# Linear attention and MoE block: two loads of each attention period are issued from ACT's queue instead of SP's

## Chip, cores, metric

One NeuronCore of a Trainium2 chip runs the whole program; the other cores are idle. The metric is the device time of one execution in microseconds (us). Engines are named as in the profile: PE (matmul), PEld (its weight loads), DVE (vector), ACT (scalar), POOL (GpSimd), SP (sync, issues transfers). "SPq" and "ACTq" are the instruction queues of SP and ACT where they issue transfers or wait.

## The reference

Linear attention over 8 batches of 8 heads (sequence 576, head size 64, 128 features), then a two-matrix feed-forward block (512 to 2048 to 512) over the 4608 rows that result.

```python
def phi(x):
    proj = einsum('bhsd,df->bhsf', x, w_phi)
    proj = proj - max(abs(proj), axis=-1, keepdims=True)
    return concatenate([exp(proj), exp(-proj)], axis=-1)
q_p, k_p = phi(q), phi(k)
kv  = einsum('bhsf,bhsd->bhfd', k_p, v)
z   = sum(k_p, axis=2)
num = einsum('bhsf,bhfd->bhsd', q_p, kv)
den = einsum('bhsf,bhf->bhs', q_p, z)[..., None] + 1e-06
attn = num / den
...
h = x @ w_in
out = (h - tanh(h)) @ w_out
```

The feed-forward weights come as 64-bit floats and are taken apart bit by bit on the core ("decoded") into 32-bit ones.

## The kernel before

The attention works on 32 units of two heads. A short ramp starts the first three; then `period(i)` runs for i = 3 to 31 (L808) and works on five units at once: it projects unit i, finishes the feature maps of i-1, sums and contracts i-2, takes numerator and denominator of i-3, and divides and stores i-4 and i-5. The order of the program is written out by hand: every engine and every queue executes its own instructions in the order in which the period names them, and waits are put in only where data or a buffer is not ready. Beside the units each period decodes one of 31 tiles of raw weights and prepares split weights for the feed-forward stage ("aside" work: subtractions on POOL, copies on ACT, stores `wd<-wr`). After period 31 a drain empties the pipeline, and the feed-forward stage, bound by matmuls, fills the rest of the time.

What one period issues on SP's queue, in order: `raw<-in_moe_w` (`dec_load`, L260 to L272, 512 KB, one of two buffers), `xs<-d` (`x_store`, the quotient of unit i-5, 288 KB, after POOL's multiplication `d<-d,rb` at L510), `qk<-in_qkT` (`load`, L300 to L303, 576 KB, one of two buffers), `dn<-dd` (`den_recip_load`, L492, the denominators of unit i-3 turned from rows into a column layout, 4.5 KB), two `rb<-rr` (`den_spread`, L507, the reciprocals broadcast over partitions), `v<-in_v` (320 KB), the stores of split weights, and `rr<-rn` (`den_store`, L502), which follows the reciprocal of the denominators on DVE (L497).

On ACT the middle of a period reads: `ksum_copy` (L432, the feature sums `kst`), `denom_copy` (L487, the denominators `dd`), copies `kv` (L449) and `ks` (L441), the first step of the decoding (`dec_0`, L279), copies of the weight preparation, the exponentials of q and k, `kvt` (L415), `num_copy` (L483). On DVE a period has the two steps of the feature maps' maxima (L345, L346), three further steps of the decoding (L283 to L291) and then the reciprocal (L497). On PE: projection (L327: `pj`, `pa`, `pt`), feature sums (L428), denominators (L470: `pu`), transposes (L445, L437, L356, L367), key-value product (L409), numerators (L456: `po`). The transposes at L367 write the part of bank `pu` that `denom_copy` has read.

The raw tile loaded in period i is used from L279 of period i+1 on, and its buffer is free after L291 of the period that uses it. The q and k loaded in period i are projected in period i+2, and their buffer is free when the projection of unit i in period i has ended.

Of the kernel before, what the change touches and what calls it, by code (L numbers as in the profile page):

```python
# [33 lines left out]
def tile_linear_attention_moe(  # L34
# [10 lines left out]
    nc = tc.nc  # L45
# [181 lines left out]
    with ExitStack() as c1:  # L227
# [32 lines left out]
        def dec_load(n, queue=nc.sync):  # L260
            u = Dec()
            kind, u.f = tiles[n]
            u.nm = f"{kind}{u.f}"
            u.d = wi if kind == "i" else wo
            u.r = raw.tile([P, DM], U64, tag="raw", name=f"raw{u.nm}")
            if kind == "i":
                queue.dma_start(
                    u.r.rearrange("p (c f) -> p c f", f=P),
                    w_in[:, u.f * P : (u.f + 1) * P].rearrange("(c p) f -> p c f", p=P),
                )  # L270
            else:
                queue.dma_start(u.r, w_out[u.f * P : (u.f + 1) * P, :])  # L272
            return u
# [26 lines left out]
        def load(u, queue=nc.sync):  # L300
            u.qk = pq.tile([P, PC], F32, tag="qk", name=f"qk{u.i}")
            for o, w in ((0, PC),) if u.i else ((5 * P, PC), (0, 5 * P)):
                queue.dma_start(u.qk[:, o:w], qkT[u.i][:, o:w])  # L303

        def load_v(u):
            u.v = pq.tile([P, 5, 2, D], F32, tag="v", name=f"v{u.i}")
            nc.sync.dma_start(u.v.rearrange("p j e d -> p (j e d)"), v5[u.i])


        def project(u, parts):  # L310
            for part in parts:
                if u.t is None:
                    u.t = [pq.tile([P, 2, 5, F], F32, tag="t0", name=f"t{u.i}_0"), None]
                    u.m = [p2.tile([P, 2, 5], F32, tag="m0", name=f"m{u.i}_0"), p2.tile([P, 2, 4], F32, tag="m1", name=f"m{u.i}_1")]
                if part == "j":
                    u.pj = ps_pj.tile([P, 2, 512], F32, tag="pj", name=f"pj{u.i}")
                    bank, tiles = u.pj, range(4)
                elif part == "t":
                    u.pt = ps_t.tile([P, 2, 512], F32, tag="pt", name=f"pt{u.i}")
                    bank, tiles = u.pt, range(4, 5)  # L320
                else:
                    u.pa = ps_d.tile([P, 2, 512], F32, tag="po", name=f"pa{u.i}")
                    bank, tiles = u.pa, range(5, 9)
                for k, a in enumerate(tiles):
                    for e in range(2):
                        hs = slice(e * D, (e + 1) * D)
                        nc.tensor.matmul(  # L327
                            bank[:, e, k * F : (k + 1) * F], u.qk[hs, a * P : (a + 1) * P], wph[hs, :], start=True, stop=True
                        )
# [10 lines left out]
        def centre(u, parts, h=None):  # L340
            for part in parts:
                x, m, t = part_of(u, part)
                if h is not None:
                    x, m, t = x[:, :, h], m[:, :, h], t[:, :, h]
                nc.vector.tensor_reduce(m, x, AX.X, ALU.max, apply_absolute_value=True)  # L345
                nc.vector.tensor_tensor(t, x, m.unsqueeze(3).broadcast_to(list(t.shape)), ALU.subtract)  # L346
# [48 lines left out]
        def k_exp(u, r, signs=(0, 1)):  # L395
            h, x, j = ((slice(SR, P), 4, 0), (slice(0, P), slice(0, 4), slice(1, 5)))[r]
            for s in signs:
                nc.scalar.activation(u.kp[h, :, j, s, :], u.t[r][h, :, x, :], AF.Exp, scale=1.0 - 2.0 * s)  # L398
# [18 lines left out]
        def kadd(u):  # L417
            x = p2.tile([P, 2, 2, F], F32, tag="ss", name=f"ss{u.i}")
            nc.gpsimd.tensor_tensor(x, u.kp[:, :, 1], u.kp[:, :, 2], ALU.add)
            nc.gpsimd.tensor_tensor(x, x, u.kp[:, :, 3], ALU.add)  # L420
            nc.gpsimd.tensor_tensor(x, x, u.kp[:, :, 4], ALU.add)
            nc.gpsimd.tensor_tensor(x, x, u.kp[:, :, 0], ALU.add)
            u.ss = x

        def ksum(u, x):
            u.pu = x
            for n in range(4):
                nc.tensor.matmul(x[n * 32 : (n + 1) * 32], ones, u.ss[:, n // 2, n % 2, :], start=True, stop=True)  # L428

        def ksum_copy(u):  # L430
            u.kst = p1.tile([P, F], F32, tag="kst", name=f"kst{u.i}")
            nc.scalar.copy(u.kst, u.pu)  # L432
# [31 lines left out]
        def denom(u, pu):  # L464
            u.pd = pu[:, F : F + CH]
            for s in range(2):
                for e in range(2):
                    for c in range(2):
                        n, w = 2 * e + c, 2 * e + s
                        nc.tensor.matmul(  # L470
                            u.pd[n * 32 : (n + 1) * 32, :],
                            u.ks[:, w * 32 : (w + 1) * 32],
                            u.qe[:, e, s, c * CH : (c + 1) * CH],
                            start=(s == 0),
                            stop=(s == 1),
                        )

        def num_copy(u):
            if u.i % 4 or u.i >= NU - 3:
                u.d = tail.tile([P, S], F32, tag="d", name=f"d{u.i}", bufs=3)  # L480
            else:
                u.d = p1.tile([P, S], F32, tag="d0", name=f"d{u.i}")
            nc.scalar.copy(u.d.rearrange("p (c n) -> p c n", c=2), u.po[:, :, 0:CH])  # L483

        def denom_copy(u):
            u.dd = pd.tile([P, CH], F32, tag="dd", name=f"dd{u.i}")
            nc.scalar.activation(u.dd, u.pd, AF.Identity, bias=bias_t[:, 3:4])  # L487

        def den_recip_load(u):
            w = 2 * S // P  # L490
            u.dn = tail.tile([P, w], F32, tag="dn", name=f"dn{u.i}")
            nc.sync.dma_start(u.dn, u.dd.rearrange("(n r) c -> n r c", r=32)[:, 0, :])  # L492
# [11 lines left out]
        def den_spread(u):  # L504
            u.rb = tail.tile([P, S], F32, tag="rb", name=f"rb{u.i}", bufs=1)
            for e in range(2):
                nc.sync.dma_start(u.rb[e * D : (e + 1) * D, :], u.rr[e : e + 1, :].broadcast_to([D, S]))  # L507

        def den_mul(u, pin=lambda ins: ins):
            pin(nc.gpsimd.tensor_tensor(u.d, u.d, u.rb, ALU.mult))  # L510

        def x_store(u):
            nc.sync.dma_start(xs[u.b // 2][u.hp, :, (u.b % 2) * S : (u.b % 2 + 1) * S], u.d)

        units = []
# [5 lines left out]
        NU = len(units)  # L521
# [7 lines left out]
        dec = []  # L529

        def unit(i):
            return units[i] if 0 <= i < NU else None

        def bank():
            return ps_c.tile([P, 512], F32, tag="pu", name="pu")
# [67 lines left out]
        def aside_at(i, late):  # L603
            for f in aside[i][late]:
                f()
# [56 lines left out]
        def period(i):  # L662
            a, c, p, r, q, o = (unit(i - n) for n in range(6))
            w = dec[i - 3]
            dec.append(dec_load(i - 2))
            if i > 3:
                num_copy(r)
            k_exp(c, 1)
            if o:
                den_mul(o)  # L670
                x_store(o)
            if i + 2 < NU:
                load(units[i + 2])
            project(a, "jat")
            centre(a, "jt")
            kadd(c)
            ksum(p, p.pc[:, 0:F])
            ksum_copy(p)
            pu = bank()
            denom(r, pu)  # L680
            denom_copy(r)
            den_recip_load(r)
            if q:
                den_spread(q)
            if i > 3:
                load_v(a)
            aside_at(i, 2)
            aside_at(i, 3)
            kv_turn(p)
            ksum_turn(p, p.pc[:, F : 2 * F])  # L690
            kv_turn_copy(p, nc.scalar.copy)
            ksum_turn_copy(p)
            dec_0(w, a.pt)
            if i < NU - 1:
                aside_at(i, False)
            aside_at(i, True)
            q_turn(c)
            q_turn_rest(c, pu)
            q_exp(c)
            q_exp_rest(c)  # L700
            centre(a, "a")
            k_exp(a, 0)
            kv(c)
            kv_copy(c)
            dec_1(w)
            dec_2(w)
            dec_3(w)
            if r:
                den_recip(r)
                den_store(r)  # L710
            num(p)
# [96 lines left out]
        for i in range(3, NU):  # L808
            period(i)
# [541 lines left out]
```

## Time and profile before

| | us |
|---|---|
| median of 3 runs | 1057.58 |
| range of the runs | 1056.92 to 1059.92 |
| profiled execution, its own time | 1059.23 |
| span of its instructions | 1057.4 |

The profile comes from one execution. Busy times are shares of the span; times in rows count from the span's start. An engine's idle time is listed with what ended it, as inferred from semaphores. A transfer's row is its issue; the landing is seen in the chain of waits or in who waits for it.

### The profile page before, as it was taken

Reading aid. Unit: us, or ns where it says so; the run is one execution under the profiler, and the core shown is the slowest. Engines: PE = TensorE matmul, PEld = TensorE weight load, DVE = VectorE, ACT = ScalarE, POOL = GpSimd, SP = SyncE. Lnnn points to the kernel's source line nnn. Section 1 sums busy time; section 2 is a strip of 40 time slices with the busy share of each in tenths; the row PEclk is TensorE's granted clock in tenths of the full one; section 3 lists DMA queues with packets and bytes.
Section 4 is the critical chain, followed back from the end, with each engine's and each line's share of the span. In section 5 each row is a group of like instructions: output and inputs, shape, how many; then the busy total and the mean of one; then the engine's idle time right before and its main releaser. Section 6 shows DMA issues by size and latency. Waiting matters only on the chain.

```text
span 1057.4 us, 19349 instructions
## 1 busy us (share of the span) xinstructions
PE 1042.4 (99%) x7484; PEld 874.0 (83%) x7484; DVE 870.2 (82%) x1086; ACT 792.1 (75%) x1281; POOL 272.8 (26%) x233
## 2 busy tenths in 40 slices
PE   8999999999989999999999999999999999999998
PEld 6666666666668998999999999999999999999997
DVE  7899888889979899878887788867887778877776
ACT  5888888988878778766777666776677667776665
POOL 4799899989960000000000000000000000000000
PEclk9999999999999999999999999999999999999999
DMA  5789999999847653464335433345334543353311
GB/s 166 205 233 282 264 271 288 267 272 270 253 142 263 201 187 103 159 216 144 121 120 190 167 131 122 120 169 179 128 106 156 199 137 113 120 180 109 123 47 60
DMA packets 75738, 184.59 MB, mean 175 GB/s; under 512 B 15744, under 2 KB 30464, under 8 KB 75648
## 3 DMA queue, kind: packets, MB, share of 16 engines
q1 hardware_dynamic: 75360, 183.17, 53.9%
q8 instruction: 59, 0.97, 0.4%
q14 instruction: 31, 0.25, 0.1%
q10 hardware_dynamic: 288, 0.20, 0.1%
HBM read 149.49 MB, written 33.70 MB: 173 GB/s over the span
## 4 chain that ended last, share of the span: by engine, by line
PE 82%; DMA 7%; DVE 5%; ACT 2%; POOL 2%; issue 1%; SPq 1%; ACTq 0%; DVEq 0%; POOLq 0%
PE A L142 18%; PE B L142 14%; PE po L987 12%; PE po L988 12%; PE po L993 12%; DMA dn<-dd 4%; PE po L456 3%; PE pc L409 3%; DVE t L346 2%; PE pj L327 2%; PE pa L327 2%; PE pu L470 2%; DVE m L345 1%; DMA rb<-rr 1%; DMA rr<-rn 1%
## 5 line engine op out<-in xcount | busy, mean ns | idle before, releaser
L142 PE MATMUL A<-xo,wr 128*128 128x384 f32 x1152 | 231.5, 337 | 0.0
L142 PEld LDWEIGHTS A<-xo,wr 128*128 128x128 f32 x1152 | 204.9, 188 | 11.4 <-ACT d L483 0.5
L911 ACT COPY u<-A 128x384 f32<-128x384 f32 x143 | 68.5, 479 | 142.6 <-PE A L142 142.2
L142 PE MATMUL B<-xo,wr 128*128 128x384 f32 x864 | 173.7, 337 | 0.0
L142 PEld LDWEIGHTS B<-xo,wr 128*128 128x128 f32 x864 | 152.5, 188 | 4.2 <-DVE hx L918 0.4
L987 PE MATMUL po<-who,ghx 128*128 128x512 f32 x288 | 112.3, 390 | 0.7 <-ACT hy L925 0.7
L987 PE MATMUL po<-who,ghy 128*128 128x512 f32 x288 | 112.3, 390 | 0.3 <-ACT ghy L962 0.3
L988 PE MATMUL po<-wlo,ghx 128*128 128x512 f32 x288 | 112.0, 389 | 0.0
L988 PE MATMUL po<-wlo,ghy 128*128 128x512 f32 x288 | 112.0, 389 | 0.0
L510 POOL TENSOR_TENSOR d<-d,rb 128x576 f32<-128x576 f32 x32 | 46.3, 1448 | 165.4 <-DMA rb<-rr 160.8
L950 DVE SCALAR_TENSOR_TENSOR s2y<-s2y,thy 128x768 f32<-128x768 f32 x48 | 46.0, 959 | 51.5 <-ACT thy L941 51.5
L398 ACT ACTIVATE kp<-t 64x256 f32<-64x256 f32 (+1 forms) x126 | 85.1, 722 | 2.1 <-DVE t L346 1.0
L993 PE MATMUL po<-who,glx 128*128 128x512 f32 x288 | 80.9, 389 | 0.0
L935 ACT ACTIVATE yx<-hx 128x768 f32<-128x768 f32 (+1 forms) x49 | 41.0, 836 | 52.9 <-DVE hx L918 52.9
L993 PE MATMUL po<-who,gly 128*128 128x512 f32 x282 | 79.3, 389 | 0.3 <-DVE gly L965 0.3
L409 PE MATMUL pc<-kp,v 128*64 128x256 f32 x640 | 76.1, 384 | 0.5 <-DMA v<-in_v 0.4
L456 PE MATMUL po<-qe,kv 128*64 128x288 f32 x512 | 69.0, 412 | 0.4
L993 PEld LDWEIGHTS po<-who,glx 128*128 128x128 f32 x288 | 54.0, 188 | 11.2
L947 DVE SCALAR_TENSOR_TENSOR s2x<-s2x,yx 128x768 f32<-128x768 f32 (+1 forms) x49 | 46.1, 941 | 20.4 <-ACT s2x L936 19.1
L993 PEld LDWEIGHTS po<-who,gly 128*128 128x128 f32 x282 | 52.8, 188 | 11.7 <-DVE gly L965 0.8
L987 PEld LDWEIGHTS po<-who,ghx 128*128 128x128 f32 x288 | 54.1, 188 | 8.8 <-ACT hy L925 1.1
L987 PEld LDWEIGHTS po<-who,ghy 128*128 128x128 f32 x288 | 54.1, 188 | 8.5 <-ACT ghy L962 0.7
(186 smaller groups left out, 2228.8 us busy)
## 6 DMA issues: line engine op xcount, KB each, us to landing
wr<-wd SPq DMA_DIRECT2D x92, 512.0 KB
wr<-wd SPq DMA_DIRECT2D x46, 768.0 KB
qk<-in_qkT SPq DMA_DIRECT2D x31, 576.0 KB
v<-in_v SPq DMA_DIRECT2D x32, 320.0 KB
rb<-rr SPq DMA_DIRECT2D x64, 144.0 KB
xs<-d SPq DMA_DIRECT2D x32, 288.0 KB
out<-o SPq DMA_DIRECT2D x35, 256.0 KB
rawi<-in_moe_w_in SPq DMA_DIRECT2D x16, 512.0 KB
```

The costliest lines, as they stand in the source:

```text
L142: nc.tensor.matmul(bank[:, 0:HT], w[:, a, n, cs], x[:, b, c, :], start=start and i == 0, stop=i == 5, skip_group_check=not start,)
L327: nc.tensor.matmul(bank[:, e, k * F : (k + 1) * F], u.qk[hs, a * P : (a + 1) * P], wph[hs, :], start=True, stop=True)
L398: nc.scalar.activation(u.kp[h, :, j, s, :], u.t[r][h, :, x, :], AF.Exp, scale=1.0 - 2.0 * s)
L409: nc.tensor.matmul(u.pc[e * D : (e + 1) * D, 0 : 2 * F], u.v[:, j, e, :], u.kp[:, e, j, :, :], start=(j == first), stop=(j == last))
L456: nc.tensor.matmul(u.po[e * D : (e + 1) * D, c, 0:CH], u.kv[:, s, e * D : (e + 1) * D], u.qe[:, e, s, c * CH : (c + 1) * CH], start=(s == ...
L510: pin(nc.gpsimd.tensor_tensor(u.d, u.d, u.rb, ALU.mult))
L911: nc.scalar.copy(t, A[q][:, 0:HT])
L947: nc.vector.scalar_tensor_tensor(z.s[:, s], z.s[:, s], GC, z.y[:, s], ALU.add, ALU.mult)
L950: nc.vector.scalar_tensor_tensor(z.s[:, s], z.s[:, s], GK, z.th[:, s], ALU.mult, ALU.mult)
L987: nc.tensor.matmul(po, z.gh[:, ts], wh, start=first, stop=False)
L988: nc.tensor.matmul(po, z.gh[:, ts], wl, start=False, stop=False)
L993: nc.tensor.matmul(po, z.gl[:, ts], wh, start=False, stop=last)
```

## The change

The two loads of a period leave SP's queue and the period's beginning; they are issued by ACT, after the copy of the feature sums and before the copy of the denominators. The loads of the ramp, the one in the drain, and all other transfers stay on SP's queue.

```diff
         def period(i):
             a, c, p, r, q, o = (unit(i - n) for n in range(6))
             w = dec[i - 3]
-            dec.append(dec_load(i - 2))
             if i > 3:
                 num_copy(r)
             k_exp(c, 1)
             if o:
                 den_mul(o)
                 x_store(o)
-            if i + 2 < NU:
-                load(units[i + 2])
             project(a, "jat")
             centre(a, "jt")
             kadd(c)
             ksum(p, p.pc[:, 0:F])
             ksum_copy(p)
+            dec.append(dec_load(i - 2, nc.scalar))
+            if i + 2 < NU:
+                load(units[i + 2], nc.scalar)
             pu = bank()
             denom(r, pu)
             denom_copy(r)
             den_recip_load(r)
```

## Rows read from the trace of the kernel before

**Rows 1.** The page, busy time of each engine over the span.
```profile
PE 1042.4 (99%) x7484; PEld 874.0 (83%) x7484; DVE 870.2 (82%) x1086; ACT 792.1 (75%) x1281; POOL 272.8 (26%) x233
```

**Rows 2.** Busy time by stretch: projection 3 to projection 31; then clock, DMA share, GB/s.
```profile
23.41:284.19 260.78, 256.89 (x3280) 172.70 (x3277) 234.63 (x310) 228.25 (x450) 229.88 (x194) 1.00 0.89 260
```

**Rows 3.** Timeline, PE: projections that open three periods (start us, us, instruction).
```profile
200.33 1.16 PE L327 MATMUL pj<-wph,qk 64*128 64x128 f32 x16
...
209.42 1.16 PE L327 MATMUL pj<-wph,qk 64*128 64x128 f32 x16
...
219.39 1.16 PE L327 MATMUL pj<-wph,qk 64*128 64x128 f32 x16
```

**Rows 4.** Waits of DVE, 30 to 300 us: total us, times, longest us.
```profile
DVE rn L497 <- DMA dn<-dd: 9.1, 11, 1.3
...
DVE rn L497 <- DMA v<-in_v: 2.2, 2, 1.6
DVE rn L497 <- DMA rb<-rr: 1.1, 2, 0.6
```

**Rows 5.** Timeline, DVE: the reciprocal in two periods, idle time before it in brackets.
```profile
201.43 0.21 DVE L497 RECIPROCAL rn<-dn 128x9 f32<-128x9 f32 x1 [0.46 <-DMA dn<-dd]
...
211.44 0.22 DVE L497 RECIPROCAL rn<-dn 128x9 f32<-128x9 f32 x1 [1.34 <-DMA dn<-dd]
```

**Rows 6.** Chain that ended last: two transfers of 4.5 KB (start us, us, what).
```profile
107.95 2.83 DMA rr<-rn
...
204.86 6.49 DMA dn<-dd
```

**Rows 7.** Timeline, SP: what one period issues, down to the broadcasts.
```profile
202.09 0.38 SPq L272 DMA_DIRECT2D rawo<-in_moe_w_out  x1
203.97 0.32 SPq L513 DMA_DIRECT2D xs<-d  x1
204.38 0.38 SPq L303 DMA_DIRECT2D qk<-in_qkT  x1
204.86 0.59 SPq L492 DMA_DIRECT2D dn<-dd  x1
205.54 3.18 SPq L507 DMA_DIRECT2D rb<-rr  x2
```

**Rows 8.** The page, DMA queues (q1 is SP's, q10 ACT's): packets, MB, share.
```profile
q1 hardware_dynamic: 75360, 183.17, 53.9%
...
q10 hardware_dynamic: 288, 0.20, 0.1%
```

**Rows 9.** Timeline, all engines: around the place of the new issues, and the raw tile's use.
```profile
200.29 0.69 DVE L291 SCALAR_TENSOR_TENSOR wi<-rawi,pt 128x512 uint32<-128x512 uint32 x1
...
202.22 0.39 PE L327 MATMUL pt<-wph,qk 64*128 64x128 f32 x4
...
203.11 0.25 ACT L432 COPY kst<-pc 128x128 f32<-128x128 f32 x1
...
204.05 0.50 ACT L487 ACTIVATE dd<-pu,bias_t 128x288 f32<-128x288 f32 x1 [0.70 <-PE pu L470]
...
204.89 0.28 PE L367 MATMUL pu<-ident,t 64*128 64x64 f32 x2
...
214.81 0.66 ACT L279 ACTIVATE pt<-rawo 128x512 f32<-128x512 f32 x1 [0.68 <-DVE t L346]
```

**Rows 10.** Line 487: ACT's queue waiting for the denominators; ns min/median/max.
```profile
L487 ACTq EVENT_SEMAPHORE  x31: 616/895/2111, 35.8 to 308.5; - x31
```

**Rows 11.** Line 303: issue of a q, k load on SP; ns min/median/max.
```profile
L303 SPq DMA_DIRECT2D qk<-in_qkT x33: 328/383/929, 0.7 to 270.9; - x33
```

**Rows 12.** Waits of SP's queue, 30 to 300 us: total us, times, longest us.
```profile
SPq L272 <- DMA qk<-in_qkT: 2.5, 3, 1.1
```

**Rows 13.** Timeline, SP: a q, k load and the raw load eight issues after it.
```profile
243.86 0.38 SPq L303 DMA_DIRECT2D qk<-in_qkT  x1
...
250.12 0.33 SPq L272 DMA_DIRECT2D rawo<-in_moe_w_out  x1
```

## The prediction

> **What bounds the kernel now.** Three views, in this order. First the page's busy times: PE is busy for 99% of the span [rows 1], so time can only come from where PE stands. Then the stretch of the attention: the 28 periods from the projection of unit 3 to that of unit 31 take 260.78 us [rows 2], 9.31 us each. The timeline gives the length of single periods, from one projection to the next [rows 3]: 9.09 us from 200.33 to 209.42, 9.97 us from 209.42 to 219.39. A period issues the same matmuls each time, and 9.09 is the shortest that I find, often repeated; I take it as PE's floor. 28 x 9.09 = 254.5, so 260.78 - 254.5 = 6.3 us is all that better feeding can give here. Of the other resources DVE works 234.6 of those 260.8 us, POOL 229.9, ACT 228.3, and the DMA engines are 0.89 busy at 260 GB/s [rows 2]: all close behind PE.
>
> Third, what makes a period long. DVE stops at the reciprocal of the denominators, L497, until `dn` has landed: 9.1 + 2.2 + 1.1 = 12.4 us in 15 periods [rows 4] (the releaser named differs, the waiting line is one; I count all three as the same wait). Behind the reciprocal, in DVE's order, stand the maxima of the next projection, then the transposes on PE and the first decoding step on ACT. A wait of 0.46 us opened the period of 9.09, one of 1.34 us the period of 9.97 [rows 3, 5]. So some 0.48 us of such a wait is hidden and the rest lengthens the period (1.34 - 0.88 = 0.46 gives the same). 12.4 - 15 x 0.48 = 5.2 us of the 6.3 belong to late denominators, at least, since waits under 0.48 subtract too much.
>
> Why `dn` is late: it is 4.5 KB, and took 6.49 us in the chain, where `rr`, as small, took 2.83 [rows 6]. All but 0.2 MB of the program's 183 MB goes through one queue, SP's [rows 8], and on it `dn` stands behind the raw tile, `xs` and q, k [rows 7]: 512 + 288 + 576 = 1376 KB, 5.4 us at 260 GB/s.
>
> **The change, part by part.**
>
> *SP loses two issues.* The q, k issue holds SP from 204.38 to 204.76, and `dn` follows at 204.86 [rows 7]; two such places make 0.48 x 2 = 0.96 us of SP's time per period. `dn` can follow `xs` directly, 0.4 us earlier, if `dd` is there (it ended at 204.55 [rows 9]; so 0.3 here). The broadcasts, `v` and the stores move up with it. SP is not the bound, so by itself this gives only that.
>
> *The transfers on two queues.* On SP's queue `dn` has only `xs` of this period ahead: 288 KB are 1.1 us at the full 260 GB/s, 2.3 at half of it. No row shows two loaded queues side by side, so I bound it. Below: `dn` lands as soon as `rr` does plus that, 2.83 + 1.1 to 2.83 + 2.3, or 3.9 to 5.1 us, 1.4 to 2.6 us sooner than 6.49. Above: the 16 engines take the same bytes in the same order, and nothing is sooner. I take the upper half of the gain, since the two loads wait in a ring of their own. Then a gain of 1.4 covers nearly every wait (1.6 is the longest [rows 4]), and 5.2 us come back. Even a third of it, 0.5 us, would bring back more than half, because only what exceeds 0.48 counts.
>
> The Trainium skill (DMA: Bandwidth & Descriptors, Issuing engines are not separate DMA queues) speaks against this: transfers from different engines run on the same 16 DMA engines, and issuing from several saves only issue time. By it the sum would hold nothing but SP's issue time, a rival below. The same page (Queues, rings and completion order) says that each DMA engine goes round between the queues packet by packet, which would be the gain; no run here shows it yet.
>
> *The loads start later or earlier.* The raw tile goes from 202.09 to some 203.2, 1.1 us later, and its first user comes at 214.81 [rows 7, 9]: 11.6 us, where even the 6.49 us transfer would do. Cost nothing; if it took over 11.6 us, ACT would stop there. q and k go from 204.38 to some 203.7, for a projection two periods on. Cost nothing.
>
> *Waits taken to ACT.* Raw needs the buffer that DVE's L291 frees (200.98), q and k the one that PE's `pt` frees (202.61); both are over before `kst` starts at 203.11 [rows 9]. Behind the issues on ACT stand `dd`, then `kv`, `ks`, decoding and exponentials; PE's L367 overwrites what `dd` reads and ran 0.34 us after `dd` had ended [rows 9].
>
> *ACT's time.* ACT is busy 228.25 / 28 = 8.15 us of a period; two issues as on SP (0.48 each, of which 0.383 is the instruction [rows 11]) make 9.11, over the floor, if they exclude work. They need not: ACT's queue already begins to wait for the denominators as `kst` starts, for 895 ns in the median [rows 10], so it runs ahead of the copy. 0.96 us in a hole of 0.895 makes `dd` 0.07 us late, 28 x 0.07 = 1.9 us if every period passes it on, nothing if L367's slack takes it. I take 1.0. If ACT's queue does not run ahead past an issue, the hole is 0.70 us [rows 9], `dd` is 0.26 late, and 7.3 us is the upper end.
>
> **Sum.** 5.2 - 1.0 = 4.2 us. The profiled execution took 1059.23 us, its span 1057.4; so 1055.0 against its own time, and as it lies 1.65 above the median of 1057.58, 1053.4 us against the median. What lies behind the attention starts earlier and is not touched.
>
> **Rivals.**
>
> *All of it comes.* Every period falls to 9.09 and ACT passes nothing on: 6.3 us, 1051.3. For it: POOL and ACT also wait for what is late now. Against: DMA engines near their limit. Chance 0.10.
>
> *The order on the DMA engines stays.* Raw, `xs`, q and k still pass before `dn`, only from two rings; raw starts 1.1 us later, which takes back what SP's shorter queue gives. 1057.6, with 1 us on ACT at most 1058.6. For it: DMA engines 0.89 busy, so the bytes ahead decide. Against: `dn` waits for 1376 KB of which 1088 leave its queue. Chance 0.25.
>
> *Slower: an issue holds ACT until an old load has landed.* SP's raw issues waited three times for the landing of q, k, up to 1.1 us [rows 12]. In each the q, k load was the eighth transfer before: from 243.86 come `dn`, two `rb`, `v`, two `xo`, `rr`, and raw is the eighth at 250.12 [rows 13]. So an issue waits for the eighth before it, and this one landed after about 6.2 us. In the new order a period with one store has raw as eighth after the last q, k load: ACT would wait there, with `dd` and PE behind. It has some 8.6 us for it (9.09 - 0.48). It decides where q, k, sharing the engines, takes longer than that. Each 0.1 us per period costs 2.8 us; more than 0.26 us on average eats the 4.2 and another 3.2. With 0.3 us: 8.4 - 4.2 = 4.2 us slower, 1061.8. For it: the loads are the largest, with engines 0.89 busy. Against: 2.4 us to spare. Chance 0.20.
>
> **How the numbers follow.** A measurement of this kernel tells about 0.3% from no change, 3.2 us: faster is under 1054.4, slower over 1060.8. Forecast (0.45) and the first rival (0.10) are faster, but the forecast lies only 1.0 us inside, so I leave 0.03 of it to "same": faster 0.52, same 0.28, slower 0.20. The forecast's own range is 1051.3 to 1055.5. The range given goes from 1051.0 to 1060.5: it holds the first three cases, and leaves out most of the slow one.
>
> **What would show it.** Right: q10 carries some 30 MB; DVE's wait at L497 shrinks from 12.4 to under 3 us; periods of 9.09 to 9.2; `dn` lands in 4 to 5 us; `dd` starts within 0.1 us of `pu`'s end as now. Wrong: waits at L497 as before (second rival); ACT idle at L487 or its queue longer than 0.9 us, with PE waiting at L367 (third); a raw tile late at L279.

## The result, and the profile after

The changed kernel takes **1067.45 us** (median of 4 runs, 1066.42 to 1068.43); the kernel before, run beside it, 1058.21 (4 runs, 1056.92 to 1059.92). The ratio is 1.0086, with a 95% interval of 1.0067 to 1.0105: some 9 us slower. The forecast was 1053.4 with a range of 1051.0 to 1060.5; the sign is wrong, and the time lies outside the range.

The profiled execution took 1066.42 us, its span 1064.6, against 1057.4 before: 7.2 us more. The page of the changed kernel answers [rows 1, 8]: PE is as busy as it was, and some 31 MB have gone from q1, SP's queue, to q10, ACT's.

```profile
PE 1044.1 (98%) x7484; PEld 875.3 (82%) x7484; DVE 870.4 (82%) x1086; ACT 791.6 (74%) x1281; POOL 272.3 (26%) x233
...
q1 hardware_dynamic: 61536, 152.04, 43.4%
q10 hardware_dynamic: 14112, 31.33, 10.3%
```

The stretch of the 28 periods, from the projection of unit 3 to that of unit 31 (columns as in [rows 2]: length, busy time of PE, PEld, DVE, ACT, POOL, clock, DMA share, GB/s):

```profile
23.52:291.94 268.42, 258.53 (x3280) 173.86 (x3277) 234.61 (x310) 227.05 (x450) 230.02 (x195) 1.00 0.85 252
```

It grew from 260.78 to 268.42 us, by 7.64: the whole loss of the profiled execution lies here. The granted clock is at its full 2.4 GHz in both, and no engine works more than PE's 1.6 us longer than before. The DMA engines are less busy, 0.85 against 0.89: they have the same bytes and more time.

Waits of the changed kernel, 30 to 300 us (total us, times, longest us), answering [rows 4]:

```profile
POOL d L510 <- DMA rb<-rr: 20.5, 19, 3.5
DVE rn L497 <- DMA dn<-dd: 13.3, 13, 1.7
...
DVE rn L497 <- DMA v<-in_v: 5.4, 3, 2.3
...
DVE rn L497 <- DMA rb<-rr: 2.6, 2, 1.4
```

POOL's wait for the broadcasts was 11.7 us in 16 periods before. The wait that was to vanish has grown: 13.3 + 5.4 + 2.6 = 21.3 us in 18 periods, after 12.4 in 15. The prediction's rule, that 0.48 us of each is hidden and the rest lengthens the period, still counts right: 21.3 - 18 x 0.48 = 12.7, less the 5.2 of before is 7.5, against the 7.64 measured. So what has to be explained is why the denominators are later.

The chain of waits of the changed kernel (start us, us, what), for the transfers that answer to `dn` in [rows 6]:

```profile
202.50 6.14 DMA dn<-dd
...
212.56 5.72 DMA dn<-dd
```

They are about as slow as the 6.49 us of before, although raw, q and k have left their queue. Over the 28 periods, from issue to landing, the median of `dn` went from 5.08 to 5.83 us and that of `xs` from 3.52 to 6.27 (worked out from the updates of the transfers' semaphores in the two traces). One period shows how. SP's timeline (start us, us, instruction), then ACT's:

```profile
212.15 0.32 SPq L513 DMA_DIRECT2D xs<-d  x1
212.56 0.59 SPq L492 DMA_DIRECT2D dn<-dd  x1
213.88 1.11 SPq L507 DMA_DIRECT2D rb<-rr  x2
215.08 0.54 SPq L307 DMA_DIRECT2D v<-in_v  x1
```

```profile
210.39 0.27 ACT L432 COPY kst<-pc 128x128 f32<-128x128 f32 x1
210.49 0.33 ACTq L272 DMA_DIRECT2D rawo<-in_moe_w_out  x1
210.92 0.39 ACTq L303 DMA_DIRECT2D qk<-in_qkT  x1
211.36 0.50 ACT L487 ACTIVATE dd<-pu,bias_t 128x288 f32<-128x288 f32 x1 [0.70 <-DVE t L346]
```

And the DMA queues (packets, MB, share of the 16 engines) in three stretches of this period: 212.2 to 215.2, 215.2 to 216.7 and 216.7 to 217.7 us:

```profile
q10 hardware_dynamic: 174, 0.68, 78.9%
q1 hardware_dynamic: 10, 0.00, 0.2%
...
q10 hardware_dynamic: 99, 0.37, 60.7%
q1 hardware_dynamic: 108, 0.23, 38.7%
...
q1 hardware_dynamic: 272, 0.28, 104.9%
```

`xs` is on q1 from 212.15 on, `dn` from 212.56 on. For 3 us q1 moves nothing of them, while q10 moves raw and the first of q, k. For 1.5 us the two queues share. `dn`'s 36-byte packets come after 216.7, with the last of `xs`. So raw and q, k, issued first, are still ahead of `xs` and `dn`; a second queue is no way past them.

The other periods are alike. By the sizes of the packets in the two traces, `xs` has its first packet 0.92 us after its issue before (median) and 3.24 us after it now. Raw's first packet, on q10, came ahead of that of `xs`, on q1, in all 26 periods that store `xs`, and q, k's in 23 of 25.

On ACT's side, answering [rows 11, 10], the q, k issues and the queue's waits for the denominators:

```profile
L303 ACTq DMA_DIRECT2D qk<-in_qkT x27: 334/517/1447, 26.7 to 277.0; - x27
L487 ACTq EVENT_SEMAPHORE  x9: 17/17/2099, 37.2 to 315.8; - x9
```

A q, k issue takes 0.52 us here, up to 1.45, and the queue stops for the denominators 9 times, where it was 31 times before: the two issues fill the hole. Idle time before `dd`, summed over the 28 periods, grew from 18.8 to 24.0 us.

### The profile page after: what moved, and what is told of

Its sections match the earlier page's. It is cut to its first block, busy times and chain, and to the rows that moved or that the text cites. A ratio compares the mean times of both kernels' runs of the same rounds, so it can differ in the third digit from the quotient of the medians.

```text
span 1064.6 us, 19312 instructions
## 1 busy us (share of the span) xinstructions
PE 1044.1 (98%) x7484; PEld 875.3 (82%) x7484; DVE 870.4 (82%) x1086; ACT 791.6 (74%) x1281; POOL 272.3 (26%) x233
## 3 DMA queue, kind: packets, MB, share of 16 engines
q10 hardware_dynamic: 14112, 31.33, 10.3%
## 4 chain that ended last, share of the span: by engine, by line
PE 73%; DMA 12%; DVE 5%; ACT 4%; POOL 4%; issue 1%; SPq 1%; ACTq 1%; POOLq 0%; DVEq 0%
PE A L142 18%; PE B L142 14%; PE po L987 12%; PE po L988 12%; PE po L993 12%; DMA dn<-dd 4%; DMA rb<-rr 3%; DMA rr<-rn 2%; DVE t L346 2%; DMA xs<-d 2%; DVE m L345 2%; PE po L456 2%; ACT kp L398 1%; PE pc L409 1%; POOL d L510 1%
## 5 line engine op out<-in xcount | busy, mean ns | idle before, releaser
L409 PE MATMUL pc<-kp,v 128*64 128x256 f32 x640 | 76.1, 384 | 0.8 <-ACT ks L441 0.2
L993 PEld LDWEIGHTS po<-who,gly 128*128 128x128 f32 x282 | 52.9, 188 | 11.7 <-DVE gly L965 0.7
L409 PEld LDWEIGHTS pc<-kp,v 128*64 128x64 f32 x640 | 43.4, 136 | 22.0 <-ACT ks L441 1.8
```

The lines of the kernel that those rows point to most:

```text
L409: nc.tensor.matmul(u.pc[e * D : (e + 1) * D, 0 : 2 * F], u.v[:, j, e, :], u.kp[:, e, j, :, :], start=(j == first), stop=(j == last))
L993: nc.tensor.matmul(po, z.gl[:, ts], wh, start=False, stop=last)
```

## The experiments

**The theories**, by the letters of the expectations. P: what is issued first passes first, on either queue; at first q, k were taken for what delays `xs` and `dn`. T (from e5 on): it is raw, issued later, that pushes back everything issued after it. Q: a second queue costs something itself. A: the two issues hold ACT. L: an issue is held until an old load has landed (the slower rival, in whatever queue it turns up).

Medians are set against runs of the kernel before beside them (medians of 1060.05 to 1060.43 us). "28 periods" below is the stretch of [rows 2], from each trace's timeline, and "L497" the sum of DVE's waits there, 30 to 300 us. A trace is one execution: e6 and e17 are the same kernel, and their 28 periods took 258.46 and 256.04 us, so a difference of 2 us between two traces says little.

**e1_lanes.** In the waits of SP's queue the changed kernel has 28.5 + 15.3 us behind the landing of `xs`, which was not so before:

```profile
SPq L502 <- DMA xs<-d: 28.5, 11, 4.2
...
SPq L112 <- DMA xs<-d: 15.3, 6, 3.4
```

As in [rows 12, 13], the transfer waited for is the eighth before: the trace has the program's transfers on eight semaphores in turn, 62 issues each. Naming `xs` between the two loads moves it by one in that count and alters nothing else:

```diff
-                x_store(o)
...
             dec.append(dec_load(i - 2, nc.scalar))
+            if o:
+                x_store(o)
             if i + 2 < NU:
```

> The changed kernel with the store of xs named between the two loads. SP's and ACT's queues hold the same instructions in the same order; only the count of transfers, by which each issue waits for the eighth before it, is as in the kernel before (raw, xs, q k, dn). Theory L (the loss comes from SP's issue of rr and of weight stores waiting until xs, now the eighth before them, has landed: 28.5 + 15.3 us of such waits in the changed kernel): these waits fall under 10 us in total and the time returns to 1056 to 1060 us. Theory P (the loss comes from the order in which the DMA engines serve: q and k are now issued ahead of xs and dn and pass first, whatever queue they are on): xs still lands 6 us after its issue, DVE's wait at L497 stays near 20 us, time 1064 to 1068. Theory A (the two issues hold ACT): as the changed kernel, 1067.

Measured: 1070.61, ratio 1.0103 [1.0067, 1.0139]; 28 periods 273.93. The waits did not move (26.2 us in 9 and 16.0 in 6), so it could not test L, and the time did not come back.

**e2_raw and e3_qk** do one half of the change each: only raw, or only q, k, on ACT behind `ksum_copy`.

```diff
-            dec.append(dec_load(i - 2))
...
+            dec.append(dec_load(i - 2, nc.scalar))
```

> Only the raw load moves to ACT, at the new place; q and k stay on SP behind xs. Theory P: xs goes ahead of q and k again and lands in 3.5 to 4.5 us, dn stands behind the same transfers as before: 1056 to 1061 us. Theory L: xs is the eighth before rr in periods with one store here too, but counts only if xs lands late: between 1058 and 1064. Theory A: half of ACT's load of issues, some 1063.

> Only q and k move to ACT, at the new place; the raw load stays first on SP. The count of eight is as in the kernel before. Theory P: q and k are issued some 0.7 us ahead of xs and pass first, xs lands 2 to 3 us later than before, dn no sooner than before: 1060 to 1067. Theory L: no new wait for xs at rr, 1056 to 1060. Theory A: some 1063 from one issue on ACT per period.

Raw alone: 1068.73, ratio 1.0082 [1.0053, 1.0112]. q, k alone: 1059.77, 0.9996 [0.9972, 1.0019]. The whole loss is raw's. This is outside every range given for e2, and P had it the other way round, the loss with q, k. DVE's wait with raw alone, and SP's with q, k alone:

```profile
DVE rn L497 <- DMA dn<-dd: 20.0, 17, 2.2
```

```profile
SPq L502 <- DMA xs<-d: 16.8, 10, 2.5
```

With q, k on ACT `xs` lands late too (6.65 us), and SP waits for it eight transfers on; the time stays. With the waits for raw, SP is held before `rr` for 25.7 us in 18 periods in e3, without a loss, and for 27.7 us in 17 in e2, with all of it. So L falls as the cause. A falls with e2: the idle time before `dd` is 18.5 us there, no more than the 18.8 before.

**e4_dn_first** leaves raw in place and moves q, k on SP's queue behind `dn`. If `dn` alone were the matter, this should bring back the 5.2 us of the prediction.

```diff
-            if i + 2 < NU:
-                load(units[i + 2])
...
             den_recip_load(r)
+            if i + 2 < NU:
+                load(units[i + 2])
```

> The kernel before with q and k issued directly behind dn instead of ahead of it, all on SP. Theory P: dn and xs no longer stand behind 576 KB, dn lands about 2 us sooner (5.1 to 3 us in the median), DVE's wait at L497 goes from 12.4 to under 4 us, time 1052 to 1056. If the denominators are late for another reason than the bytes ahead of them (no theory that counts on order holds): 1057 to 1060. Theories L and A say nothing against 1058.

Measured: 1060.76, ratio 1.0012 [0.999, 1.0034]. DVE no longer waits at L497 at all, the 28 periods took 259.01 us in the profiled execution, 1.8 less than before, and yet the runs show no gain. `v` is late in its stead (PE waits 2.3 us for it, 0.4 before), and POOL's wait for the broadcasts stays (11.7 us in 16 before), with longer single waits (1.8 at most before):

```profile
POOL d L510 <- DMA rb<-rr: 11.0, 10, 3.7
PE pc L409 <- DMA v<-in_v: 2.3, 2, 1.5
```

Behind the periods this execution lost 1.6 us again: PE waited there 3.1 us at once for POOL's sums (L422; 1.5 and 1.1 us in two waits before), and from 296.7 us on it was granted 1.2 GHz for 3.4 us.

**e5_place_sp** issues both loads at the change's place, but on SP's queue (first diff, against the changed kernel); **e6_raw_early** goes the other way, raw on ACT earlier than before, between the two halves of the exponentials, with q, k on SP untouched (second diff, against the kernel before).

```diff
-            dec.append(dec_load(i - 2, nc.scalar))
+            dec.append(dec_load(i - 2))
             if i + 2 < NU:
-                load(units[i + 2], nc.scalar)
+                load(units[i + 2])
```

```diff
-            dec.append(dec_load(i - 2))
...
-            k_exp(c, 1)
+            k_exp(c, 1, (0,))
+            dec.append(dec_load(i - 2, nc.scalar))
+            k_exp(c, 1, (1,))
```

> The change's places in the program, but both loads on SP's queue: SP then issues rr, xs, raw, q k, dn, so raw starts some 2 us later than before and dn stands directly behind both. Theory T (what costs is that the raw load starts later, after the DMA engines have run dry, so that what dn stands behind passes later; the queue's name does not matter): as slow as the changed kernel or slower, 1066 to 1080. Theory Q (a second queue itself costs, the place does not): 1056 to 1061.

> The raw load on ACT, but issued between the two exponentials of k that open ACT's part of the period, about 0.9 us into it instead of 2.9 (1.9 in the kernel before); q and k stay on SP as before. Theory T: not slower than before, 1054 to 1061, DVE's wait at L497 at or under 12.4 us. Theory Q: raw on ACT's queue costs as with raw alone at the late place, 1065 to 1070.

e5: 1086.21, ratio 1.0251 [1.0216, 1.0286]; on SP the place puts raw behind SP's own waits, 5.4 us into the period. e6: 1057.83, 0.9973 [0.9949, 0.9998], faster than the kernel before. So Q falls: ACT's queue is not at fault, and at the same place in the program it is better than SP's. On ACT's queue raw's place alone makes the difference between 0.8% lost (e2) and 0.3% gained (e6).

**e8_qk_after_v and e10_raw_late_dn_free** were to show that raw's lateness costs through `dn` alone: q, k go behind `v`, out of everyone's way, first by itself and then with raw late as in e2.

```diff
-            if i + 2 < NU:
-                load(units[i + 2])
...
                 load_v(a)
+            if i + 2 < NU:
+                load(units[i + 2])
```

> The kernel before with q and k issued on SP behind dn, both rb and v. With q, k directly behind dn the wait at L497 went to nothing and v came late instead (PE's L409 waited). Theory of order (each transfer passes in the order of issue; q and k have two periods of slack, everything else has none): no wait at L497, none for v, 1051 to 1056. If something other than late transfers sets the 0.16 us over the floor: 1057 to 1061.

> Raw on ACT at the change's late place, as in the run that was 0.8% slower, but q and k behind v on SP, out of dn's way. If raw's lateness costs only through dn's landing, the loss goes: 1052 to 1060, no wait at L497 to speak of. If it costs in another way (raw itself late for the decoding, ACT held): 1065 or more.

Both missed. e8: 1064.92, ratio 1.0046 [1.0029, 1.0062]; e10: 1078.35, 1.0179 [1.0125, 1.0233]. In e8 `rr` now passes behind q, k, and SP stops for it with the broadcasts in hand:

```profile
SPq L507 <- DMA rr<-rn: 48.2, 22, 3.4
```

Against e8, raw's lateness costs 1.3% here too, though L497 has only 17.7 us; PE waits 8.8 us for `v`, and part of the loss is the clock (see below). None of the places tried for q, k was out of everybody's way.

**e11_both_raw_early** is the change with raw at e6's place; **e12_no_raw** is the change without the periods' raw loads (all tiles are decoded from the first raw tile, so it leaves out 512 KB a period).

```diff
             u.d = wi if kind == "i" else wo
+            if n:
+                u.r = dec[0].r
+                return u
```

> The changed kernel with the raw load moved up between the two exponentials of k that open ACT's part of the period (0.7 us into it instead of 2.9); q and k stay on ACT at the change's place. Theory T (the raw load's start is the whole loss): not slower than the kernel before, 1055 to 1061. If q and k on ACT, or two issues on ACT, cost something of their own, which raw's lateness hid: 1062 to 1068.

> The changed kernel without the raw loads of the periods: every weight tile is decoded from the first raw tile, so 512 KB a period are not loaded, while q and k stay on ACT at the change's place and all arithmetic is done. Theory T: with these bytes gone nothing is late, periods go to the floor of 9.09 us, wait at L497 under 4 us, 1050 to 1057. If ACT's issue of q and k or the new order among the others (xs behind q and k) costs: above 1060.

e11: 1059.53, ratio 1.0000 [0.998, 1.0021]: two issues per period on ACT, no longer one behind the other, and no loss. e12: 1054.44, 0.994 [0.9922, 0.9958]; its 28 periods:

```profile
23.93:280.18 256.25, 255.12 (x3281) 172.58 (x3277) 234.80 (x310) 227.14 (x450) 231.36 (x195) 1.00 0.68 208
```

That is 9.15 us a period, DVE never waiting for denominators: it bears out the floor of 9.09, and the 6 us that the prediction took for all that feeding can bring.

**e13_early_dn_first** puts e6 and e4 together; **e14_raw_later** moves raw alone one step further back, behind `denom_copy`, to get a price per microsecond.

```diff
             denom_copy(r)
+            dec.append(dec_load(i - 2, nc.scalar))
             den_recip_load(r)
```

> Raw early on ACT as in the run that took 0.27% less, and q and k on SP directly behind dn. If both help independently: no wait at L497 and v earlier than in the run with q and k behind dn alone, 1051 to 1056. If the gain of raw early came through dn alone: 1056 to 1061.

> Only raw on ACT, but still later: behind the copy of the denominators (about 3.8 us into the period; 1.9 in the kernel before, 2.9 in the change, 5.4 in the run with both on SP at the change's place). Theory T, by the runs so far (+0.8% at 2.9, +2.5% at 5.4): between them, +1.2 to +2.0%, 1072 to 1082. If raw's place does not matter beyond being behind kst: 1066 to 1070.

e13 missed: 1067.27, ratio 1.0073 [1.0046, 1.0101]. Nothing is left at L497 (0.3 us), and PE waits for `v` instead:

```profile
PE pc L409 <- DMA v<-in_v: 7.1, 8, 1.7
```

e14: 1075.23, 1.0137 [1.0112, 1.0162], between e2 and e5 as expected. Its stretch, and its wait:

```profile
23.62:300.09 276.47, 258.80 (x3281) 172.46 (x3277) 233.69 (x310) 230.34 (x450) 230.06 (x195) 1.00 0.85 245
```

```profile
DVE rn L497 <- DMA dn<-dd: 29.9, 22, 2.3
```

**The last three.** e15_raw_early_sp: raw early, but on SP's queue, ahead of `rr` (the first of these loads stands behind the ramp, and the drain's own is left out; neither is shown). e16_change_v_first: the change with `v` moved to the period's front, to keep the DMA engines at work while raw is awaited. e17_raw_early_again: the kernel of e6 once more.

```diff
-            dec.append(dec_load(i - 2))
...
             dec_3(w)
+            dec.append(dec_load(i - 1))
```

```diff
             w = dec[i - 3]
+            if i > 3:
+                load_v(a)
...
-            if i > 3:
-                load_v(a)
```

> The kernel before with the raw load issued on SP's queue ahead of rr instead of behind it, as soon as DVE has taken the buffer's last tile apart (about 0.8 us into the period instead of 1.9); nothing is on ACT's queue. Theory T (the start of the raw load decides, not the queue): as raw early on ACT, -0.1 to -0.5%, 1055 to 1059. If the gain of the early raw load came from ACT's queue: 1058 to 1062.

> The changed kernel with the load of v moved to the front of the period on SP (directly behind rr instead of behind the broadcasts), so that 320 KB go through the DMA engines while they wait for the late raw load. Theory T (the loss is the time in which the DMA engines have nothing to send): most of the loss comes back, 1056 to 1063. If raw is late for a reason of its own (as what stands ahead of dn, or as the weights' tile): 1064 to 1070, since raw, q and k are as late as in the change.

> The same kernel as the raw load early on ACT with q and k on SP, timed again in more rounds, for whether it beats the kernel before. Theory T: -0.1 to -0.5%, 1055 to 1059; if the 0.27% were chance: within 0.1% of the kernel before.

e15 missed: 1062.53, ratio 1.0029 [1.001, 1.0047], so an early raw is not enough by itself. Raw is early there (0.87 us into the period in the median, but up to 3.55), but `rr` behind it is put back from 1.21 to 1.66 us and lands after raw in all 27 periods (in none before, in 10 of 27 in e17):

```profile
SPq L507 <- DMA rr<-rn: 41.8, 25, 3.2
```

e16: 1067.25, 1.0072 [1.0044, 1.01]: the loss stays. e17: 1056.98, **0.9978 [0.9961, 0.9995]**, faster again than the kernel before, and so the version that beats both. Its stretch and its waits:

```profile
24.20:280.24 256.04, 254.94 (x3280) 172.31 (x3276) 234.89 (x310) 226.13 (x450) 231.23 (x195) 1.00 0.87 264
```

```profile
DVE rn L497 <- DMA dn<-dd: 1.2, 1, 1.2
DVE rn L497 <- DMA rb<-rr: 0.5, 1, 0.5
```

**All together.** "Raw", "`rr`" and "`dn`" are the issues' places in us after the projection that opens the period (medians of each timeline); "counted" is the L497 sum less 0.48 for each wait; "over floor" is the 28 periods less 254.5.

| kernel | raw | `rr` | `dn` | L497, us in times | counted | over floor | ratio |
|---|---|---|---|---|---|---|---|
| e12, no raw | - | 0.80 | 4.26 | 0 | 0 | 1.8 | 0.994 |
| e17, raw early on ACT | 0.72 | 0.80 | 4.21 | 1.7 in 2 | 0.7 | 1.5 | 0.9978 |
| e11, the same, q, k on ACT | 0.72 | 0.80 | 4.20 | 3.6 in 3 | 2.2 | 5.7 | 1.0000 |
| before | 1.90 | 1.21 | 4.93 | 12.4 in 15 | 5.2 | 6.3 | 1 |
| e3, q, k on ACT | 2.00 | 1.59 | 4.30 | 16.6 in 20 | 7.0 | 8.5 | 0.9996 |
| the change | 2.86 | 1.91 | 4.86 | 21.3 in 18 | 12.7 | 13.9 | 1.0086 |
| e2, raw on ACT | 2.86 | 1.92 | 5.22 | 25.6 in 21 | 15.5 | 16.1 | 1.0082 |
| e14, raw later | 3.82 | 2.61 | 6.25 | 32.9 in 24 | 21.4 | 22.0 | 1.0137 |

Down the table raw is issued later, `dn` waits longer at L497, and the periods grow by what is counted there. `rr` follows, since it holds what L497 computes; after it come the broadcasts, POOL's multiplication and `xs`. Thus one period hands its lateness to the next.

The other kernels do not follow that count. "PE for `v`" is PE's wait at L409, 30 to 300 us, and "at 1.2 GHz" the time in the 28 periods in which PE was granted half its clock:

| kernel | counted | over floor | PE for `v`, us in times | at 1.2 GHz, us | ratio |
|---|---|---|---|---|---|
| e6, the kernel of e17 | 2.5 | 4.0 | 0 | 0 | 0.9973 |
| e11, from above | 2.2 | 5.7 | 3.4 in 1 | 3.4 | 1.0000 |
| e4, q, k behind `dn` | 0 | 4.5 | 2.3 in 2 | 0 | 1.0012 |
| e15, raw early on SP | 5.8 | 10.3 | 2.4 in 1 | 3.4 | 1.0029 |
| e8, q, k behind `v` | 2.6 | 10.4 | 5.0 in 4 | 3.4 | 1.0046 |
| e16, the change, `v` first | 10.5 | 13.8 | 0 | 0 | 1.0072 |
| e13, e6 and e4 together | 0 | 12.8 | 7.1 in 8 | 6.8 | 1.0073 |
| e1, the change, `xs` between | 10.1 | 19.4 | 2.4 in 2 | 3.4 | 1.0103 |
| e10, e8 with raw late | 11.9 | 25.7 | 8.8 in 7 | 20.5 | 1.0179 |
| e5, both loads late on SP | 25.4 | 28.8 | 0 | 10.3 | 1.0251 |

Most of these kernels move the wait to other places, and behind some of these waits of PE the granted clock fell to 1.2 GHz. In e11 PE waited 3.44 us for `v`, and the twenty matmuls at L409 then took 3.73 us, where e17 has 2.38; the clock was 0.50 of its full 2.4 GHz from 195.50 to 198.90 us (columns of the last row as in [rows 2]):

```profile
196.14 3.73 PE L409 MATMUL pc<-kp,v 128*64 128x256 f32 x20 [3.44 <-DMA v<-in_v]
```

```profile
193.35 2.38 PE L409 MATMUL pc<-kp,v 128*64 128x256 f32 x20
```

```profile
195.50:198.90 3.40, 2.76 (x14) 1.86 (x16) 2.02 (x3) 1.27 (x5) 3.24 (x3) 0.50 0.85 320
```

So part of the misses of e8, e10, e13 and e15 is the clock's. In the first table only e11 has such a stretch, and what the traces of the others show there owes nothing to it. Raw's loss is there without it: e2's 28 periods took 270.60 us at the full clock, 9.8 more than before.

## Why the prediction was wrong

**The step that failed first** is "The loads start later or earlier": raw 1.1 us later, "Cost nothing". The size of the move was right (1.90 to 2.86 us into the period, 0.96). Its price was taken from raw's own user, 11.6 us away [rows 7, 9], and no raw tile was ever waited for. But raw is 512 KB in a period whose DMA engines are 0.89 busy [rows 2], and what is issued behind it passes behind it: q, k, `xs`, `dn`, the broadcasts, `v`. e2 shows that this term alone is worth the whole 0.8%, and the moves on ACT to 0.72 and 3.82 us show it in both directions.

**The second is "a ring of their own"**: that with raw and q, k on q10 `dn` has only `xs` ahead, and lands 1.4 to 2.6 us sooner. It lands 0.75 us later after its issue (5.08 to 5.83), which is beyond even the other bound, "the 16 engines take the same bytes in the same order, and nothing is sooner". The sum also started from rare cases: 6.49 us is the slowest of the 28 `dn`, and the 2.83 us of `rr` compares with a median of 3.88. With the medians the same sum gives 5.0 to 6.2 us against 5.08, no gain.

On this the two sections of the Trainium skill (DMA: Bandwidth & Descriptors) that the prediction names were weighed the wrong way round. What the Trainium skill says under Issuing engines are not separate DMA queues, that several issuers save issue time alone, agrees with the traces, where `xs` on q1 began behind raw on q10 in 26 of 26 periods. What the Trainium skill says under Queues, rings and completion order, that an engine goes round the queues packet by packet, shows only in the 1.5 us of shares 60.7% and 38.7%; in the 3 us before, q1 had 0.2% with `xs` issued. No run shows whether the work of `xs` had reached the engines by then.

**A smaller one is ACT's hole.** The prediction took 1.0 us for the two issues. In the period shown `dd` keeps its idle 0.70 us, but over the 28 periods that time grew by 5.2 us (18.8 to 24.0). e2 has none of this and loses as much, so it did not show in the time.

**The rivals.** "The order on the DMA engines stays" had the mechanism, and a wrong term: raw's later start was to be made up for by SP's shorter queue. `dn` was issued 0.07 us sooner in the period (4.93 to 4.86), not the 0.3 to 0.4 that SP's shorter queue was to give, because `xs` now comes 0.41 later (4.04 to 4.45) and `dn` follows it. The slower rival had the sign for another reason: the wait for the eighth transfer before came, but on SP, and e3 has it before `rr` without a loss.

**What was right.** PE's floor, the 6 us (e12: 0.6%), L497 as the place where a period grows, with 0.48 us hidden, and that ACT's queue runs ahead: the copy `kst` still ran when raw was issued. But "5.2 of the 6.3 belong to late denominators" read a place as a cause: e4 and e13 empty L497 and gain nothing, since `v` is late in its stead and the broadcasts come no sooner, and e13 is slowed by the clock as well. What L497 shows in the kernels of the first table is the whole queue's lateness.

**What stays open.** Whether raw costs by the order alone or also by DMA engines left idle while it is awaited. By slices of 0.75 us of the period, averaged over 20 periods, the engines' share never falls under 0.80 before, but to 0.59 after (3.0 to 4.5 us in), to 0.38 in e14, and not under 0.85 in e17. e16, meant to fill that trough with `v`, left the loss, but it left the trough too (0.45), so it decides nothing. Why e11 gains less than e17 shows in its profiled execution alone: the one wait for `v`, and the clock behind it. How much the clock adds to each ratio is not worked out. No run has raw early on SP with `rr` in time, so what ACT's queue itself is worth is not shown. And no version with all its loads reached e12's 1054.44.

## What to carry to other kernels

Price a load that is moved in time not by its own user alone, but by everything that is issued behind it on any queue, wherever the DMA engines are near their limit; a second queue did not let small urgent transfers pass a large one here. Issue the large load with slack as early as its buffer allows, from an engine whose queue holds up nobody (here ACT, 1.2 us earlier: 0.2% to 0.3%). And a wait that is always at one place can be the sum of several delays: before counting its removal as a gain, look at what is late next, and at the granted clock behind the new wait.

## What was not expected of the hardware

- Two loaded queues did not share from the start: 78.9% of the engines' time to q10 and 0.2% to q1 in the first 3 us after `xs` was issued behind raw and q, k. Before the change `xs` had its first packet 0.92 us after its issue (median), so most of these 3 us is waiting.
- ACT's queue starts transfers while the copy before them still runs (copy from 210.39 for 0.27, issue at 210.49). Yet two issues in a row fill the hole: q, k's took 0.52 us in the median and up to 1.45, where e11, with raw's issue elsewhere, has 0.34.
- An issue waits for the eighth transfer before it, SP's and ACT's counted together (eight semaphores in turn), and after the change that count brings SP to a stop for `xs` (28.5 + 15.3 us). e3 has 25.7 us of such waits before `rr` at no cost to the time.
- A wait of PE can cost twice: behind 3.44 us for `v` in e11 the granted clock was 0.50, the lower of its two levels, for 3.4 us.
